# Gated attention plus Mish layer: another table of order rules, and another opening for the first K and Q

## The chip, the cores and the metric

The kernel runs on one core of one Trainium2 chip, in one launch. The metric is the device time of one execution in microseconds (us), and the median of the runs is what counts. The engines are named as in the profile: PE is TensorE's matrix unit (PEld its weight loads), DVE is VectorE, ACT is ScalarE, POOL is GpSimd, SP issues most DMAs. PSUM, where matmuls write, has eight banks of 512 float32 columns for each of its 128 partitions.

## The reference, cut to what matters

```python
def _A_ref(x, wqkv, wo):            # S = 2048 rows, D = 640, H = 32 heads of Dh = 20
    qkv = (x @ wqkv).reshape(B, S, 3, H, Dh) ...
    scores = einsum("bhqd,bhkd->bhqk", q, k) * Dh ** -0.5
    o = einsum("bhqk,bhkd->bhqd", softmax(scores), v)
    return o.reshape(B, S, D) @ wo
def _B_ref(x, w1, b1, w2):          # F = 1536
    h = x @ w1 + b1
    return (h * tanh(softplus(h))) @ w2          # Mish
g = sigmoid((x * gate_w).sum(-1, keepdims=True))
return g * _A_ref(A_x, ...) + (1 - g) * _B_ref(A_x, ...)
```

There are 32 heads x 2048 x 2048 scores, and each needs one exponential.

## The kernel before

**Units of work.** Heads are taken four at a time (`p`, 8 of them), queries 512 at a time (`qc`, 4 of them): 32 groups `G`. A group has 16 sets `j` of 128 keys, and a set has four score columns, one for each head, of 128 keys x 512 queries: 2048 columns in all, each one matmul (`score`, L1265) into one PSUM bank. Four such matmuls use different rows of the PE array (each 32 deep), so that several run side by side.

**Two ways to an exponential.** Most columns go to ScalarE: `emit_s` puts the scores of two or three columns into neighbouring banks and `emit_exp` (L1315) takes one ACTIVATE over them, a *pair* (1024 elements) or a *triple* (1536). The other sets are "drawn" for VectorE by `d_take`: `d_unit` (or `d_pair`, or two powers joined by `both`) writes scores into spare banks and `power_of` (L474) turns them into exponentials as an integer multiply and add whose bits are read as bf16. Such a set is used three times, with two shifted copies against rescaled values `VD`: a shift is one instruction on VectorE (L605) or four parts on GpSimd (L573). So a drawn set costs three value products where another set costs one.

**Value products.** `emit_pv` (L1358) issues four matmuls for a set, 21 columns of values and ones for each of the four heads, into four column strips of bank 7 (`acc`). When a group is complete, `normalise` transposes the sums on VectorE (L1380), takes reciprocals, multiplies on GpSimd (L1401) and stores the result for the last projection. The very last group is finished on VectorE alone (`ends`).

**Everything else is cut into chains.** Projections of q, k and v, the two matmuls of the Mish layer, the output projection and the transposes of x are `Chain` objects: lists of pieces (four matmuls side by side in four column strips of the array, L638) with an eviction by VectorE at the end. Mish itself is one ACTIVATE over 6144 elements, two in a batch, two batches (L926).

**What sets the order.** The program is straight-line, and the order on each engine is chosen when it is built, by a planner in the kernel's own Python: it steps a model clock, and `step_pe`, `step_act`, `step_dve` and `step_pool` choose the next instruction of each engine. On the chip each engine then runs its list in order, and waits on semaphores. `step_pe` decides by the fields of `rule` whether to issue the next scores (`S`), value products (`V`), a chain's piece (`F`) or scores for VectorE alone: for example how many banks to leave free (`KEEP3`), how many drawn sets may be open (`NOPEN`) or belong to one group (`LEAD`), how many ready value products are worth a change (`VMIN`, `PVMAX`), whether GpSimd takes a shift (`PS`, `PB`), whether two powers are joined (`MERGE`). `PLAN` (L175 and on) changes these fields while the work goes on; its keys are progress in groups, from 0 to 32:

```python
while plan and prog[0] >= plan[0]:
    vars(rule).update(PLAN[plan.pop(0)])
```

**The opening** is written by hand. Four row blocks of x are loaded on SP's and ScalarE's queues, then the weights of the first four heads (`load_first(1)` for K, `load_first(0)` for Q), `w_top` (48 more columns for K's padding) and `wv0` (the first value weights). x is transposed on TensorE, K's weights are padded into `wkp` (L366, L1474) and Q's into `wqp`, and ten matmuls for each make the first 512 columns of K and Q (L1484): for each of five row blocks of weights one matmul of 256 columns into one bank and one into another. VectorE copies one half (L1491), ScalarE the other (L1492). Then the first scores follow, and the planner's order begins.

**The end** is written by hand too: 24 matmuls for the last 512 rows (L1822), evictions and stores. `closing`, a flag, is set when the sums of the last group are transposed; while it is set, `step_dve` takes only work of the highest priority.

Of the kernel before, what the change touches and what calls it, by code (L numbers as in the profile page):

```python
# [9 lines left out]
P = 128  # L10
# [54 lines left out]
def kernel(  # L65
# [12 lines left out]
    nc = tc.nc  # L78
    _, S, D = A_x.shape
    F = B_w1.shape[1]  # L80
    H = 32
    DH = D // H
    KT = D // P
    FT = F // P
    NS = S // P
    QC = 512
# [88 lines left out]
    PLAN = {  # L175
        0.0: {'AHEAD': 5000.0, 'BEHIND': 6000.0, 'D2': 1.0, 'DQ': 2, 'DQ3': 0, 'DQ4': 0, 'ETIGHT': 1, 'HEAT': 0.7, 'HROOM': 100.0, 'KEEP3': 3, 'LEAD': 5, 'LOW': 0.5, 'MARGIN': 0.0, 'MERGE': 0, 'NEAR': 99, 'NOPEN': 5, 'PAIR': 0, 'PB': 3000.0, 'PS': 0, 'PVMAX': 4, 'Q3': 3, 'ROOM': 200.0, 'SWTH': 250.0, 'TWO': 9, 'VF': 0, 'VMIN': 1, 'WAIT1': 0.0, 'WAIT2': 6000.0, 'WAITU': 0.0},
        0.5: {'DQ4': 1, 'NEAR': 9, 'WAIT2': 100000.0},
        1.5: {'DQ3': 3, 'ETIGHT': 0, 'HEAT': 0.9, 'VMIN': 3},
        2.0: {'DQ4': 2, 'NEAR': 5, 'PS': 1, 'ROOM': 100.0, 'VMIN': 2, 'WAITU': 100000.0},
        2.5: {'AHEAD': 1000.0, 'Q3': 2},  # L180
        3.5: {'AHEAD': 2000.0, 'NEAR': 7, 'Q3': 3, 'SWTH': 520.0, 'WAIT1': -2000.0},
        4.0: {'MARGIN': 30.0, 'NEAR': 99, 'PVMAX': 2, 'VF': 2, 'VMIN': 1},
        4.5: {'ETIGHT': 1, 'TWO': 2, 'VMIN': 3},
        5.0: {'KEEP3': 1, 'LEAD': 4, 'LOW': 0.47, 'NOPEN': 4, 'Q3': 1, 'SWTH': 600.0, 'WAIT2': 3000.0},
        5.5: {'HROOM': -100.0, 'KEEP3': 3, 'LOW': 0.53, 'NEAR': 12, 'PVMAX': 3, 'VMIN': 2},
        6.0: {'PVMAX': 2},
        6.5: {'HEAT': 0.7, 'PS': 2},
        7.0: {'DQ3': 2, 'NOPEN': 5, 'TWO': 9, 'VMIN': 1},
        7.5: {'PB': 6000.0},
        8.0: {'LEAD': 6, 'WAIT2': 30000.0},  # L190
        8.5: {'HROOM': 100.0, 'MERGE': 1, 'NEAR': 9, 'Q3': 3, 'VF': 0, 'WAITU': -200000.0},
        9.0: {'D2': 0.5, 'HEAT': 0.8, 'MERGE': 0, 'WAITU': 100000.0},
        9.5: {'AHEAD': 3000.0, 'MERGE': 1, 'SWTH': 250.0, 'WAIT1': 0.0},
        10.0: {'PVMAX': 4, 'VF': 2},
        10.5: {'HEAT': 0.9},
        11.0: {'KEEP3': 1, 'ROOM': 300.0},
        11.5: {'KEEP3': 2, 'ROOM': 100.0},
        12.0: {'D2': 0, 'DQ': 1, 'LOW': 0.41, 'MERGE': 0, 'SWTH': 450.0},
        12.5: {'NOPEN': 3, 'Q3': 1},
        13.0: {'Q3': 3},  # L200
        14.0: {'HROOM': -200.0, 'LOW': 0.47, 'WAIT2': 100000.0},
        14.5: {'NOPEN': 2},
        15.0: {'HEAT': 0.7},
        15.5: {'HEAT': 0.9},
        16.0: {'DQ3': 0, 'DQ4': 0, 'HROOM': -100.0},
        17.0: {'PB': 3000.0},
        17.5: {'D2': 0.5, 'PB': 6000.0, 'TWO': 2},
        18.0: {'ROOM': 200.0},
        19.0: {'LOW': 0.6, 'NOPEN': 5},
        19.5: {'DQ3': 2, 'DQ4': 3, 'ETIGHT': 0, 'KEEP3': 1, 'LOW': 0.53, 'TWO': 1},  # L210
        20.0: {'DQ4': 1, 'MARGIN': 60.0, 'MERGE': 1, 'TWO': 2, 'WAIT1': -2000.0, 'WAITU': 0.0},
        20.5: {'NEAR': 99, 'PB': 3000.0, 'SWTH': 380.0},
        21.0: {'DQ4': 2, 'KEEP3': 3, 'NEAR': 7, 'PVMAX': 3},
        21.5: {'ETIGHT': 1, 'MERGE': 0, 'PB': 6000.0, 'Q3': 2, 'WAIT2': 30000.0},
        22.0: {'HROOM': 0.0, 'ROOM': 100.0},
        23.0: {'HROOM': -200.0, 'TWO': 1},
        23.5: {'PVMAX': 2},
        24.0: {'MARGIN': 30.0, 'NOPEN': 2, 'TWO': 9},
        25.0: {'NOPEN': 4, 'PB': 1500.0, 'PVMAX': 4, 'ROOM': 200.0, 'SWTH': 520.0, 'WAIT2': 100000.0},
        25.5: {'LEAD': 5, 'PB': 3000.0, 'WAIT2': 3000.0},  # L220
        26.0: {'HROOM': 100.0, 'ROOM': 100.0, 'TWO': 2},
        26.5: {'HROOM': -200.0, 'PVMAX': 2},
        27.0: {'KEEP3': 2, 'WAIT1': 0.0, 'WAITU': 100000.0},
        27.5: {'LOW': 0.44, 'PVMAX': 4, 'Q3': 3},
        28.0: {'DQ': 2, 'KEEP3': 3, 'MARGIN': 0.0},
        28.5: {'LOW': 0.38, 'TWO': 9, 'WAIT2': 30000.0},
        29.5: {'DQ': 1, 'DQ4': 1, 'NOPEN': 2, 'PS': 0, 'Q3': 1, 'WAIT2': 100000.0},
    }

    x2d = A_x[0]  # L230
# [9 lines left out]
    xT = consts.tile([P, KT, S], BF16, tag="xT")  # L240
    VA = consts.tile([P, NS, H, DH + 1], BF16, tag="VA")
    wv0 = work.tile([P, KT, 4 * DH + 1], BF16, tag="bl1", name="wv0")
# [7 lines left out]
    wqp = consts.tile([P, KT, 4, 32], BF16, tag="wqp")  # L250
    wkp = consts.tile([P, KT, 4, 32], BF16, tag="wkp")
# [4 lines left out]
    allb = psum.tile([P, 8, QC], F32, tag="Sp", name="Sp")  # L256
# [3 lines left out]
    def bank_ap(tag, shape, dtype=F32):  # L260
        ap = allb[:, tag, :]
        if dtype != F32:
            ap = ap.bitcast(dtype)
        if len(shape) == 3:
            return ap[:, 0 : shape[1] * shape[2]].rearrange("p (a b) -> p a b", b=shape[2])
        return ap[:, 0 : shape[1]]
# [9 lines left out]
    wrows = A_wqkv.rearrange("(kt p) c -> p kt c", p=P)  # L276
# [8 lines left out]
    KTOP = D - KPAD  # L285
# [9 lines left out]
    w_top = work.tile([P, KT, KPAD], BF16, tag="bl0", name="w_top")  # L295
# [20 lines left out]
        eng = nc.sync if u % 2 == 0 else nc.scalar  # L316
        eng.dma_start(out=xs[0][:, u, :], in_=x2d[u * P : (u + 1) * P, :])
    load_first(1, nc.sync)
    nc.scalar.dma_start(out=w_top[:, :, :], in_=wrows[:, :, D + KTOP : 2 * D])
    load_first(0, nc.scalar)  # L320
    nc.sync.dma_start(out=wv0[:, :, 0 : 4 * DH], in_=wrows[:, :, 2 * D : 2 * D + 4 * DH])

    def load_x(c):
        nc.sync.dma_start(  # L324
# [40 lines left out]
    def pad_copy(eng, dst, src):  # L365
        eng.tensor_copy(  # L366
            out=dst[:, :, :, 0:DH], in_=src.rearrange("p k (h d) -> p k h d", d=DH)
        )
# [4 lines left out]
    NG = len(groups)  # L373
# [16 lines left out]
    act_q = deque()  # L390
    pool_q = []
    two_port = [0.0]
    closing = [False]
    seq = [0]
    free = {"PE": 0.0, "ACT": 0.0, "DVE": 0.0, "POOL": 0.0}
    mode = [None]
# [975 lines left out]
    def normalise(G, ready):  # L1372
# [2 lines left out]
        st = {}  # L1375

        def a(t):
            closing[0] = G == NG - 1
            st["T1"] = work.tile([P, NS, 32], F32, tag=f"T1_{i}", name="T1")
            nc.vector.transpose(out=st["T1"][:, :, :].rearrange("p b r -> p (b r)"), in_=acc[:, :])  # L1380

# [30 lines left out]
        def ends(t):  # L1412
            st["O"] = work.tile([P, QC], BF16, tag=f"O{i}", name="O")
            for h in range(2):
                q = slice(h * QC // 2, (h + 1) * QC // 2)
                b_ = slice(h * NS // 2, (h + 1) * NS // 2)
                nc.vector.tensor_tensor(
                    out=T2[i][:, q].rearrange("p (b r) -> p b r", r=32)[:, :, 0:DH],
                    in0=st["T1"][:, b_, 0:DH],
                    in1=st["rec"][:, b_].unsqueeze(2).to_broadcast([P, NS // 2, DH]),  # L1420
                    op=ALU.mult,
                )
                nc.vector.transpose(out=st["O"][:, q], in_=T2[i][:, q])
            o_last[p] = st["O"]
            closing[0] = False

        def c_done(t):
            if kept:
# [46 lines left out]
        out=wkp[:, :, :, DH:32], in_=w_top[:, :, :].rearrange("p k (h d) -> p k h d", h=4)  # L1475
    )
    pad_copy(nc.vector, wqp, w_first[0][:, :, :])
    kT[0] = kTb[0]
    qT[0] = qTb[0]
    h_ = QC // 2  # L1480
    for w, dst, two in ((wkp, kT[0], (1, 4)), (wqp, qT[0], (5, 0))):
        for kt in range(KT):
            for h in range(2):
                nc.tensor.matmul(  # L1484
                    allb[:, two[h], 0:h_],
                    lhsT=w[:, kt, :, :].rearrange("p h d -> p (h d)"),
                    rhs=xT[:, kt, h * h_ : (h + 1) * h_],
                    start=(kt == 0),
                    stop=(kt == KT - 1),
                )  # L1490
        nc.vector.tensor_copy(out=dst[:, 0:h_], in_=allb[:, two[0], 0:h_])  # L1491
        nc.scalar.copy(out=dst[:, h_:QC], in_=allb[:, two[1], 0:h_])  # L1492
    for p in range(NQ - NSB, NQ):
        tag = "wqp" if p < NQ - 1 else f"wo{p}"
        wo_pad[p] = consts.tile([P, D], BF16, tag=tag, name=f"wo{p}")
# [236 lines left out]
    def step_dve(t):  # L1732
        best = None
        for it in dve_q:
            if it[1] <= t and (it[0] == 0 or not closing[0]) and (it[6] is None or it[6](t)):
                due = it[1] + (WAIT0, rule.WAIT1, rule.WAIT2, MWAIT)[it[0]]
                if it[0] == 3:
                    due = min(due, it[7] + WAIT3)
                if it[6] is not None and it[0] == 2 and cur["G"] > pv_G[0]:
                    due = min(due, it[1] + rule.WAITU)  # L1740
                rank = (due, it[2])
                if best is None or rank < best[0]:
                    best = (rank, it)
        if best is None:
            return None
        best = best[1]
        dve_q.remove(best)
        _, _, _, cost, fn, done, _, _ = best
        if rule.MERGE and best[2] in powers:
            o = beside(best, t)  # L1750
            if o:
                dve_q.remove(o)
                both(best, o, t)
                cost = 1134.0
                for x in (best, o):
                    x[5](t + cost + DVE_TAIL + SEM)
                return cost
        if best[0] == 2 and best[6] is not None:
            cost += max(free["POOL"] - t, 0.0)
            two_port[0] = t + cost  # L1760
        fn(t)
        if done:
            done(t + cost + DVE_TAIL + SEM)
        return cost
# [117 lines left out]
```

## Time and profile before

| | us |
|---|---|
| median of 3 runs (723.77 to 724.47) | 724.05 |
| the profiled execution: its time | 725.01 |
| the profiled execution: first to last instruction (span) | 723.2 |
| busy: PE / ACT / DVE / POOL | 706.3 / 704.3 / 619.6 / 430.4 |
| first exp starts / last exp ends | 9.67 / 714.45 |

Times within the profile are counted from the first instruction. "Busy" is the union of an engine's instructions; consecutive ones overlap on ACT and PE, so a busy engine can still have lost time: the step from start to start tells more than the duration. "Idle before" in a row is what the engine waited ahead of such instructions, with who ended the wait. The granted TensorE clock is 0.999 of full speed over the whole span.

### The profile page before, as it was taken

Reading aid. Unit: us, or ns where it says so; the run is one execution under the profiler, and the core shown is the slowest. Engines: PE = TensorE matmul, PEld = TensorE weight load, DVE = VectorE, ACT = ScalarE, POOL = GpSimd, SP = SyncE. Lnnn points to the kernel's source line nnn. Section 1 sums busy time; section 2 is a strip of 40 time slices with the busy share of each in tenths; the row PEclk is TensorE's granted clock in tenths of the full one; section 3 lists DMA queues with packets and bytes.
Section 4 is the critical chain, followed back from the end, with each engine's and each line's share of the span. In section 5 each row is a group of like instructions: output and inputs, shape, how many; then the busy total and the mean of one; then the engine's idle time right before and its main releaser. Section 6 shows DMA issues by size and latency. Waiting matters only on the chain.

```text
span 723.2 us, 24705 instructions
## 1 busy us (share of the span) xinstructions
PE 706.3 (98%) x10256; PEld 232.5 (32%) x10256; DVE 619.6 (86%) x1042; ACT 704.3 (97%) x735; POOL 430.4 (60%) x697
## 2 busy tenths in 40 slices
PE   8899999999999999999999999999999999999997
PEld 4433332222222443332332222222243333333332
DVE  5389999887788779889988899898889988988997
ACT  6899999999999999999999999999999999999996
POOL 2002675565797767778787778667984456663000
PEclk9999999999999999999999999999999999999999
DMA  9511122122321201111131223231231131132111
GB/s 246 178 22 38 30 56 44 33 62 59 85 43 32 68 27 28 14 32 27 50 84 34 41 47 70 60 67 38 44 57 31 34 50 35 29 60 45 20 36 38
DMA packets 123313, 37.87 MB, mean 52 GB/s; under 512 B 90880, under 2 KB 122640, under 8 KB 123200
## 3 DMA queue, kind: packets, MB, share of 16 engines
q1 hardware_dynamic: 121600, 35.80, 22.8%
q8 instruction: 80, 1.31, 0.7%
q10 hardware_dynamic: 1600, 0.49, 0.3%
q14 instruction: 33, 0.27, 0.1%
HBM read 22.29 MB, written 11.48 MB: 47 GB/s over the span
## 4 chain that ended last, share of the span: by engine, by line
PE 62%; ACT 23%; issue 5%; DVE 4%; SPq 2%; DMA 2%; POOL 0%; ACTq 0%; POOLq 0%
PE Sp L1265 22%; ACT E L1315 20%; PE Sp L1358 20%; PE Sp L638 20%; DVE T L474 2%; ACT big L926 1%; DMA w_sb<-in_B_w_dram 1%; DVE T L605 1%; SPq L291 1%; SPq L304 1%; DMA big<-in_A_x_dram 1%; PE Sp L1822 0%; SPq L708 0%; SPq L324 0%; ACT L1315 0%
## 5 line engine op out<-in xcount | busy, mean ns | idle before, releaser
L1315 ACT ACTIVATE E<-Sp 128x1024 bf16<-128x1024 f32 x717 | 672.6, 1077 | 6.3 <-PE Sp L1265 5.9
L573 POOL TENSOR_TENSOR T<-T,step_t 128x256 int32<-128x256 int32 x652 | 401.1, 649 | 107.9 <-PE Sp L1358 71.5
L474 DVE TENSOR_SCALAR T<-Sp 128x512 int16<-128x512 f32 (+1 forms) x587 | 389.1, 686 | 62.3 <-PE Sp L1265 57.7
L1265 PE MATMUL Sp<-qT,kT 32*128 32x512 bf16 x2048 | 290.9, 384 | 8.0 <-ACT E L1315 3.7
L1265 PEld LDWEIGHTS <-kT 32*128 32x128 bf16 x2048 | 74.5, 91 | 267.0 <-issue 262.0
L1358 PE MATMUL Sp<-E,VA 128*21 128x512 bf16 x1456 | 138.0, 383 | 0.4 <-DVE T L1380 0.4
L1401 POOL TENSOR_TENSOR T<-T,rec 128x320 bf16<-128x320 f32 x31 | 25.1, 809 | 167.0 <-DVE rec L1394 140.0
L1358 PE MATMUL Sp<-T,VD 128*21 128x512 bf16 x1184 | 112.2, 382 | 0.5 <-DVE T L605 0.5
L605 DVE TENSOR_SCALAR T<-T 128x2048 int16<-128x2048 int16 x133 | 105.2, 797 | 1.5 <-PE Sp L1358 0.5
L638 PE MATMUL Sp<-xT,w1t 128*32 128x512 bf16 x960 | 76.8, 383 | 0.2
L638 PE MATMUL Sp<-w_sb,big 128*32 128x320 bf16 x1536 | 74.3, 301 | 0.3 <-DVE st L742 0.3
L1358 PEld LDWEIGHTS <-VA 128*21 128x21 bf16 x2048 | 44.4, 90 | 72.5 <-issue 64.5
L1358 PE MATMUL Sp<-T,VA 128*21 128x512 bf16 x592 | 57.4, 383 | 0.0
L638 PE MATMUL Sp<-xT,ws 128*32 128x512 bf16 x720 | 55.9, 382 | 0.5 <-DVE T L474 0.5
L638 PEld LDWEIGHTS <-big 128*32 128x32 bf16 x1536 | 35.4, 96 | 25.9 <-issue 15.8
L1358 PEld LDWEIGHTS <-VD 128*21 128x21 bf16 x1184 | 28.4, 90 | 37.6 <-issue 32.2
L892 DVE TENSOR_SCALAR big<-Sp,b1f 128x512 bf16<-128x512 f32 x48 | 35.6, 742 | 2.1 <-PE Sp L638 1.9
L638 PE MATMUL Sp<-wv,xT 128*32 128x81 bf16 (+2 forms) x960 | 34.6, 258 | 1.3 <-DVE T L474 1.3
L638 PE MATMUL Sp<-wo_sb,od 128*32 128x320 bf16 (+1 forms) x608 | 32.3, 302 | 0.0
L742 DVE CAST st<-Sp 128x512 bf16<-128x512 f32 x36 | 24.5, 681 | 5.3 <-PE Sp L638 5.3
L638 PEld LDWEIGHTS <-w1t 128*32 128x32 bf16 x960 | 19.0, 94 | 26.3 <-issue 22.4
L826 DVE CAST VA<-Sp 128x80 bf16<-128x80 f32 (+2 forms) x48 | 16.2, 372 | 10.1 <-PE Sp L638 10.1
(74 smaller groups left out, 205.7 us busy)
## 6 DMA issues: line engine op xcount, KB each, us to landing
w1t<-in_B_w_dram SPq DMA_DIRECT2D x24, 320.0 KB
q_dram<-st SPq DMA_DIRECT2D x20, 128.0 KB
out_dram<-ot SPq DMA_DIRECT2D x16, 160.0 KB
qT<-q_dram SPq DMA_DIRECT2D x124, 20.0 KB
o_dram<-T SPq DMA_DIRECT2D x120, 20.0 KB
kT<-k_dram SPq DMA_DIRECT2D x28, 80.0 KB
k_dram<-st SPq DMA_DIRECT2D x16, 128.0 KB
big<-in_A_x_dram SPq DMA_DIRECT2D x3, 640.0 KB
```

The costliest lines, as they stand in the source:

```text
L291: eng.dma_start(out=t[:, :, :], in_=wrows[:, :, c0 : c0 + P])
L474: nc.vector.tensor_scalar(out=dst.bitcast(I16), in0=src, scalar1=inv_sqrt_dh * LOG2E * 128.0, scalar2=127.0 * 128.0 + BETA, op0=ALU.mult, ...
L573: nc.gpsimd.tensor_tensor(out=tile_[:, :].bitcast(I32)[:, k * n : (k + 1) * n], in0=d["T"][:, :].bitcast(I32)[:, k * n : (k + 1) * n], in1 ...
L605: nc.vector.tensor_scalar(out=tile_[:, :].bitcast(I16), in0=d["T"][:, :].bitcast(I16), scalar1=float(SHIFT[i]), scalar2=None, op0=ALU.add,)
L638: nc.tensor.matmul(out_[k : k + 32], lhsT=lhsT[:, k : k + 32], rhs=rhs, tile_position=(0, k), **kw)
L742: nc.vector.tensor_copy(out=res["st"][:, :], in_=ps[:, :])
L826: nc.vector.tensor_copy(out=VA[:, sts[i], h0 : h0 + nh, 0:DH], in_=ps[:, i, 0:n].rearrange("p (h d) -> p h d", d=DH),)
L892: nc.vector.tensor_scalar(out=big[:, slot.tag, (ft % 2) * QC : (ft % 2 + 1) * QC], in0=ps[:, :], scalar1=b1f[:, ft : ft + 1], scalar2=None ...
L1265: nc.tensor.matmul(ps_cols, lhsT=kT[p][32 * t_ : 32 * t_ + 32, j * P : (j + 1) * P], rhs=qT[G][32 * t_ : 32 * t_ + 32, :], tile_position=( ...
L1315: nc.scalar.activation(E[:, x : x + n, :], ps, ACT.Exp, scale=inv_sqrt_dh,)
L1358: nc.tensor.matmul(acc[32 * t_ : 32 * t_ + DH + 1, :], lhsT=lhsT, rhs=rhs, start=(pv_done[G] == 0), stop=(pv_done[G] == pv_total[G] - 1), ...
L1401: nc.gpsimd.tensor_tensor(out=T2[i][:, :].rearrange("p (b r) -> p b r", r=32)[:, :, 0:DH], in0=st["T1"][:, :, 0:DH], in1=st["rec"][:, :].u ...
```

## The change

`PLAN` is replaced from progress 1.0 on (the entries for 0.0 and 0.5 stay). `closing` goes. In the opening, `w_top` is loaded on SP's queue behind K's weights, and the first value weights on ScalarE's queue behind Q's; K and Q are made by five matmuls of 512 columns each, into one bank each (6 and 2), and both engines copy their half out of that bank. Line numbers move by 6 (L1265 becomes L1271) and by 4 near the end.

```diff
-        1.5: {'DQ3': 3, 'ETIGHT': 0, 'HEAT': 0.9, 'VMIN': 3},
-        2.0: {'DQ4': 2, 'NEAR': 5, 'PS': 1, 'ROOM': 100.0, 'VMIN': 2, 'WAITU': 100000.0},
-        2.5: {'AHEAD': 1000.0, 'Q3': 2},
...
-        29.5: {'DQ': 1, 'DQ4': 1, 'NOPEN': 2, 'PS': 0, 'Q3': 1, 'WAIT2': 100000.0},
+        1.0: {'DQ4': 3, 'VMIN': 2, 'WAITU': 100000.0},
+        1.5: {'DQ4': 2, 'PS': 2, 'PVMAX': 3},
+        2.0: {'DQ4': 1, 'PS': 1, 'PVMAX': 4, 'VF': 1, 'WAIT1': -2000.0},
...
+        31.5: {'BEHIND': 3000.0, 'DQ4': 1, 'ETIGHT': 0, 'HROOM': 100.0, 'LEAD': 5},
...
     load_first(1, nc.sync)
-    nc.scalar.dma_start(out=w_top[:, :, :], in_=wrows[:, :, D + KTOP : 2 * D])
     load_first(0, nc.scalar)
-    nc.sync.dma_start(out=wv0[:, :, 0 : 4 * DH], in_=wrows[:, :, 2 * D : 2 * D + 4 * DH])
+    nc.sync.dma_start(out=w_top[:, :, :], in_=wrows[:, :, D + KTOP : 2 * D])
+    nc.scalar.dma_start(out=wv0[:, :, 0 : 4 * DH], in_=wrows[:, :, 2 * D : 2 * D + 4 * DH])
...
-            closing[0] = G == NG - 1
...
-            closing[0] = False
...
+    sb = [bank_ap(g, [P, QC]) for g in (6, 2)]
     kT[0] = kTb[0]
     qT[0] = qTb[0]
-    h_ = QC // 2
-    for w, dst, two in ((wkp, kT[0], (1, 4)), (wqp, qT[0], (5, 0))):
+    for w, dst, k in ((wkp, kT[0][:, 0:QC], 0), (wqp, qT[0][:, :], 1)):
         for kt in range(KT):
-            for h in range(2):
-                nc.tensor.matmul(
-                    allb[:, two[h], 0:h_],
-                    lhsT=w[:, kt, :, :].rearrange("p h d -> p (h d)"),
-                    rhs=xT[:, kt, h * h_ : (h + 1) * h_],
-                    start=(kt == 0),
-                    stop=(kt == KT - 1),
-                )
-        nc.vector.tensor_copy(out=dst[:, 0:h_], in_=allb[:, two[0], 0:h_])
-        nc.scalar.copy(out=dst[:, h_:QC], in_=allb[:, two[1], 0:h_])
+            nc.tensor.matmul(
+                sb[k][:, :],
+                lhsT=w[:, kt, :, :].rearrange("p h d -> p (h d)"),
+                rhs=xT[:, kt, 0:QC],
+                start=(kt == 0),
+                stop=(kt == KT - 1),
+            )
+        h_ = QC // 2
+        nc.vector.tensor_copy(out=dst[:, 0:h_], in_=sb[k][:, 0:h_])
+        nc.scalar.copy(out=dst[:, h_:QC], in_=sb[k][:, h_:QC])
...
-            if it[1] <= t and (it[0] == 0 or not closing[0]) and (it[6] is None or it[6](t)):
+            if it[1] <= t and (it[6] is None or it[6](t)):
```

What the two programs hold, as their lists of instructions show (no time is in these):

| engine, instruction | before | after |
|---|---|---|
| ACT exp over 1024 / 1536 / 512 | 693 / 23 / 1 | 688 / 24 / 0 |
| DVE power over 512 / over 1024 | 582 / 5 | 578 / 11 |
| DVE shift / POOL parts of shifts | 133 / 652 | 135 / 660 |
| PE sets of four value matmuls | 808 | 812 |
| PE runs of scores; of these with five or more | 711; 5 | 713; 2 |
| PE matmuls for the first K and Q | 20 of 256 columns | 10 of 512 columns |

From the 24th run of scores on, the order of TensorE differs, and with it the others.

## The prediction

> **What bounds the kernel now.** I read the page's busy shares first, then ScalarE's groups by form, its timeline, the waits from 50 us on, TensorE's timeline, and last the opening.
>
> ```profile
> PE 706.3 (98%) x10256; PEld 232.5 (32%) x10256; DVE 619.6 (86%) x1042; ACT 704.3 (97%) x735; POOL 430.4 (60%) x697
> ```
>
> Two engines are full at once. ScalarE's time is nearly all exps, and its groups split them by width:
>
> ```profile
> L1315 ACT ACTIVATE E<-Sp 128x1024 bf16<-128x1024 f32 x693 | 644.4, 1064 | 6.2 <-PE Sp L1265 5.9 <-PE Sp L1358 0.2
> L1315 ACT ACTIVATE E<-Sp 128x1536 bf16<-128x1536 f32 x23 | 34.2, 1487 | 0.1
> ```
>
> 693 pairs take 644.4 us, 0.930 each. One takes 1.064 from its start to its end, so neighbours overlap, and a late start of up to 0.13 us is not idle time. ScalarE's timeline gives the step when nothing is late:
>
> ```profile
> 669.92 9.27 ACT L1315 ACTIVATE E<-Sp 128x1024 bf16<-128x1024 f32 x10
> 705.65 8.80 ACT L1315 ACTIVATE E<-Sp 128x1024 bf16<-128x1024 f32 x9
> ```
>
> Ten pairs in 9.27: less the last one's 1.08, nine steps of 0.91. The second line, by the list of the order, is six pairs, two triples and the single: (8.80 - 0.67 - 6 x 0.91) / 2 = 1.34 for a triple. Over all pairs (0.930 - 0.910) x 693 = 13.9 us are lost to late scores, besides 6.2 us of open idle, most of it before 50 us: there the ACT waits after 50 us name only this.
>
> ```profile
> ACT E L1315 <- PE Sp L1265: 0.7, 3, 0.4
> ```
>
> So ScalarE is the bound, and TensorE has next to no room to be early. Its prices stand in its timeline, as differences of starts:
>
> ```profile
> 707.26 0.46 PE L638 MATMUL Sp<-wo_sb,od 128*32 128x320 bf16 x8
> 707.55 0.39 PE L1358 MATMUL Sp<-T,VD 128*21 128x512 bf16 x4
> 707.87 0.39 PE L1265 MATMUL Sp<-qT,kT 32*128 32x512 bf16 x3
> 708.19 0.40 PE L1358 MATMUL Sp<-E,VA 128*21 128x512 bf16 x4
> 708.42 0.39 PE L1358 MATMUL Sp<-T,VD 128*21 128x512 bf16 x4
> 708.74 0.39 PE L1265 MATMUL Sp<-qT,kT 32*128 32x512 bf16 x3
> ```
>
> A set of four value matmuls takes 0.22 and another 0.10 if scores follow; a run of two to four scores takes 0.32; a group of four 320-wide ones 0.14 (8 in 0.29). A run of scores with both changes is thus 0.42, and 0.93 leaves some 0.5 for other work. Priced so, and with 0.22, 0.10 and 0.07 for groups of 512, 240 and 81 columns, the order holds 683.1 us of TensorE work against 662.0 us of exps (693 x 0.91 + 23 x 1.34 + 0.6) and 26.3 us of Mish (four of 5.3 and four table loads of 1.28), 688.3 together. ScalarE is the fuller by 5.2 us; beyond that, time is lost where one exp's slot is overfull on TensorE and the next is not.
>
> **The change, part by part.** The sums go against the profiled execution, 725.01 us with a span of 723.2; the median of the three runs, 724.05, is 0.96 lower, and the difference is carried over to it.
>
> *Exps.* By the lists of both orders: pairs 693 to 688, triples 23 to 24, the single gone: -5 x 0.930 + 1.34 - 0.67 = -4.0 us on ScalarE. These eight score columns go to VectorE (592 to 600 columns: sets drawn off ScalarE 148 to 150).
>
> *TensorE.* Two more sets mean four more value sets, 808 to 812: 4 x 0.22 = 0.9. Runs of scores 711 to 713: 2 x 0.42 = 0.8. Runs of five and more, which pay twice inside, 5 to 2: -0.6, and some regrouping. The whole list gives 683.7, +0.6. At steps without loss ScalarE comes down to 688 x 0.91 + 24 x 1.34 + 26.3 = 684.5: the two are level.
>
> *VectorE.* 582 to 578 single powers (-4 x 0.681), 5 to 11 double ones (+6 x 1.216), two more shifts (+2 x 0.797): +6.2 on 619.6, that is 87%. It waits 55.1 us for scores after 50 us, which hides this; if that cover is gone, 6.2 is the most it costs. *GpSimd:* +8 x 0.649 = 5.2 us on 60%, hidden by 107.9 us of idle before such parts; else the shift is late for its value set, not for an exp.
>
> *What of the 4.0 reaches the end.* I cut both lists behind every exp and added up, piece by piece, the larger of TensorE's work and ScalarE's steps (Mish left out in both; no wait is carried from piece to piece): 717.7 before, 715.1 after (-2.6). With cuts behind every second, third and fourth exp the change is -2.9, -1.3 and -3.8; behind every eighth -0.6, every sixteenth -0.2, every 24th +0.4. Short pieces fit the kernel, which keeps two exps' scores ahead, and they average -2.65; since work can also be moved a little, I take -2.3, and the ends for the range are +0.4 and -4.0.
>
> *The opening.* It ends at 9.67 with the first exp, and it is serial:
>
> ```profile
> 6.06 0.22 DVE L1474 COPY wkp<-w_top 128x240 bf16<-128x240 bf16 x1
> 6.34 1.30 PE L1484 MATMUL Sp<-xT,wkp 128*128 128x256 bf16 x10 [0.22 <-DVE wkp L1474]
> 7.52 1.27 PE L1484 MATMUL Sp<-xT,wqp 128*128 128x256 bf16 x10
> 8.71 0.42 DVE L1491 CAST qT<-Sp 128x256 bf16<-128x256 f32 x1 [0.71 <-PE Sp L1484]
> 8.82 0.37 ACT L1492 CAST qT<-Sp 128x256 bf16<-128x256 f32 x1 [0.77 <-PE Sp L1484]
> 9.24 0.40 PE L1265 MATMUL Sp<-qT,kT 32*128 32x512 bf16 x4 [0.46 <-ACT qT L1492]
> ```
>
> The two copies of Q run side by side out of two banks. In the changed program both read one bank, and the list with its waits shows ScalarE's copy waiting for VectorE's, no longer for TensorE. The Trainium skill, "PSUM — Partial Sum Buffer", section "PSUM bank collisions raise a hardware error", says that two engines must not read one bank and quadrant at once, and that readers are included. By that rule the wait is needed and the sum stays as follows; without it the copies could run side by side and the opening would cost 0.5 less. No run here shows two engines on one bank. Price: VectorE's copy now needs all columns (8.71 becomes about 8.85), 0.42, a hand-over of about 0.06, 0.37: scores at about 9.75 instead of 9.24, +0.5. K's copies serialise too, under Q's matmuls. Ten weight loads fewer and 512 columns a matmul cost the same columns: 0, at best -0.2.
>
> w_top's load moves from ScalarE's queue, where it is issued at 1.65 behind two x loads, to SP's behind K's weights, and so to about 2.12, where the list has the value weights now. Its landing is not shown; the first weight block, issued at 1.65, is used unwaited at 5.85, 4.2 later, so about 6.3; the latest is wqp's 7.20, the landing of a block issued at 2.14. So the copy at 6.06 is late by 0 to 1.1; I take 0.2, nearest to the first. Q's weights come sooner, but Q waits for K on TensorE (7.52 follows 7.51). The gate's and values' weights move to ScalarE's queue and are wanted at 11.98: nothing. The x loads on SP stand behind a smaller block: nothing. Opening in sum +0.7, bounds +0.3 and +1.6.
>
> *The tail.* `closing` held back VectorE's other work during the last normalisation; the changed list has none left after the last transpose of the sums, but one wo eviction (0.54) just before. The last exp is a pair (1.06, was 0.67), while the shifts that held TensorE at 714.97 are gone. 0, bounds -0.4 and +0.4.
>
> Sum: -2.3 + 0.7 = -1.6: 723.4 for a profiled execution, **722.4** for the median.
>
> **Rivals.** *Full relief* (0.17): lost time stays at 0.020 a pair, the whole 4.0 comes off: 724.05 - 4.0 + 0.7 = 720.8. For it: ScalarE is the fuller engine and TensorE's list grows by only 0.6. Against it: then both are level, and every full slot counts.
>
> *TensorE becomes the bound, in uneven slots* (0.38). In pieces of 24 exps its surplus over ScalarE grows from 24.4 to 27.4 us. If that can't be moved out of its stretch, it is paid as late scores, and the exps removed were not what was waited for: 724.05 + 3.0 + 0.7 = 727.8. It decides from the point where the mean busy time of a pair passes 0.930 + (4.0 - 0.7) / 688 = 0.935, and is slower for certain above 0.937. For it: the order is another one from the 24th run of scores on, and TensorE's waits after 50 us (3.3 us for exps) leave no reserve. Against it: short pieces all shrink.
>
> *That the rules change nothing* can't be: the lists differ in nearly every line from there on.
>
> **How the numbers follow.** This kernel's runs differ by 0.7 us, and 0.2% (1.45 us) is about what can be told from no change: faster is below 722.6, slower above 725.5. The forecast (0.45) lies at the edge of faster: 0.26 faster, 0.14 same, 0.05 slower, since its terms have ends of -4.0 to +0.4 and +0.3 to +1.6; its own range is 720 to 726. Full relief gives 0.16 and 0.01; the uneven slots 0.04 same and 0.34 slower. Faster 0.42, same 0.19, slower 0.39. The range reaches below the full relief by the 2.8 us that fewer late scores could give, and above the slower rival by 0.9 for a late w_top and 0.4 for the tail: 718.0 to 729.1.
>
> **What would show it.** Right: ScalarE's pairs 688 at 0.925 to 0.935 busy each, triples 24, first exp at 10.2 to 10.6, ScalarE's copy of Q starting where VectorE's ends. Wrong: pairs above 0.937 (late scores), open ACT waits after 50 us well over 1 us, a first exp after 11 (w_top), or TensorE waiting for VectorE's powers by several us, where double powers hold two banks for 1.2 us.

## The result, and the profile after

The changed kernel takes 721.09 us (median of 20 runs, 720.49 to 724.94); the kernel before, measured beside it, 724.39 (20 runs, 723.53 to 728.46). The ratio is 0.9952, with an interval of 0.9942 to 0.9962: faster by 3.3 us by the medians, 3.5 by the ratio, half a per cent. The profiled executions stand at 725.01 before (span 723.2) and 721.08 after (span 719.3), 3.9 apart; the one of before lies above its three timed runs (723.77 to 724.47), so a part of the 3.9 may be that execution's own.

Busy time of the engines, from the page of the changed kernel:

```profile
PE 704.2 (98%) x10262; PEld 234.2 (33%) x10262; DVE 626.0 (87%) x1046; ACT 700.2 (97%) x730; POOL 440.9 (61%) x705
```

ScalarE's groups by form (count | busy, mean ns of one | idle before, with who ended it):

```profile
L1321 ACT ACTIVATE E<-Sp 128x1024 bf16<-128x1024 f32 x688 | 640.5, 1078 | 5.6 <-PE Sp L1271 3.8 <-PE Sp L1364 1.1
L1321 ACT ACTIVATE E<-Sp 128x1536 bf16<-128x1536 f32 x24 | 36.6, 1523 | 0.4 <-PE Sp L1271 0.4
```

A pair takes 640.5 / 688 = 0.931 us of busy time; before it was 0.930. The exps that went took their full price with them, and a pair loses no more to late scores than before. All exps together, where overlaps count once, are busy 668.6 us after 672.6, so -4.0.

The waits from 50 us on, ScalarE's and TensorE's (total, times, longest):

```profile
PE Sp L1271 <- ACT E L1321: 1.8, 8, 0.4
PE Sp L1364 <- DVE T L1385: 1.3, 2, 0.8
ACT E L1321 <- PE Sp L1364: 1.1, 2, 0.9
ACT E L1321 <- PE Sp L1271: 0.9, 3, 0.4
```

and TensorE's longest group before:

```profile
PE Sp L1265 <- ACT E L1315: 3.3, 10, 0.5
```

TensorE waits less for exps to free a bank (1.8 us against 3.3), and up to the last exp neither engine waits longer than 0.9 us at once.

The opening, from the timeline (start, duration, engine, line, then the idle time and who ended it):

```profile
6.60 0.22 DVE L1478 COPY wkp<-w_top 128x240 bf16<-128x240 bf16 x1 [0.77 <-DMA w_top<-in_A_wqkv_dram]
6.88 1.25 PE L1487 MATMUL Sp<-xT,wkp 128*128 128x512 bf16 x5 [1.14 <-DVE wkp L1478]
9.32 0.42 DVE L1495 CAST qT<-Sp 128x256 bf16<-128x256 f32 x1 [0.72 <-PE Sp L1487]
9.78 0.37 ACT L1496 CAST qT<-Sp 128x256 bf16<-128x256 f32 x1 [0.78 <-DVE qT L1495]
10.20 0.40 PE L1271 MATMUL Sp<-qT,kT 32*128 32x512 bf16 x4 [0.99 <-ACT qT L1496]
```

The copy of `w_top` starts at 6.60, not at 6.06, and waits for its load. ScalarE's copy of Q starts 0.46 behind VectorE's and waits for it. The first exp starts at 10.62 instead of 9.67. Other executions with the same opening scatter: 10.54 to 11.06 in the five of e2, e6, e8, e9 and e10, and 9.47 to 10.11 in the five others with the old one (e1, e5, e7, e11, e12).

The whole stretch from the first exp's start to the last one's end (length, then busy time of PE, PEld, DVE, ACT and POOL with counts, granted clock, DMA share, GB/s):

```profile
10.62:711.06 700.44, 692.94 (x10194) 228.53 (x10194) 616.71 (x1023) 694.83 (x721) 435.67 (x691) 1.00 0.23 50
```

It was 704.78 long (9.67 to 714.45). So the 3.9 us divide into +0.95 ahead of the first exp, -4.34 in this stretch, and -0.51 behind the last exp (8.75 to 8.24: the first transpose of the last sums starts 0.48 after the last exp's end, where it was 1.01).

### The profile page after: what moved, and what is told of

Read it like the earlier page. It is cut to its first block, busy times and chain, and to the rows that moved or that the text cites. A ratio compares the mean times of both kernels' runs of the same rounds, so it can differ in the third digit from the quotient of the medians.

```text
span 719.3 us, 24738 instructions
## 1 busy us (share of the span) xinstructions
PE 704.2 (98%) x10262; PEld 234.2 (33%) x10262; DVE 626.0 (87%) x1046; ACT 700.2 (97%) x730; POOL 440.9 (61%) x705
## 4 chain that ended last, share of the span: by engine, by line
PE 67%; ACT 23%; issue 5%; DVE 2%; DMA 1%; SPq 0%; ACTq 0%; DVEq 0%
PE Sp L1271 24%; PE Sp L644 22%; ACT E L1321 21%; PE Sp L1364 21%; ACT big L932 1%; DVE T L480 1%; DMA kT<-k_dram 1%; DMA w_top<-in_A_wqkv_dram 1%; DVE T L611 0%; PE Sp L1487 0%; DVE st L748 0%; ACT L1321 0%; ACT L932 0%; SPq L777 0%; DVE VD L431 0%
## 5 line engine op out<-in xcount | busy, mean ns | idle before, releaser
L1321 ACT ACTIVATE E<-Sp 128x1024 bf16<-128x1024 f32 (+1 forms) x712 | 668.6, 1093 | 6.0 <-PE Sp L1271 4.2
L579 POOL TENSOR_TENSOR T<-T,step_t 128x256 int32<-128x256 int32 x660 | 409.7, 655 | 157.4 <-PE Sp L1364 92.3
L480 DVE TENSOR_SCALAR T<-Sp 128x512 int16<-128x512 f32 (+1 forms) x589 | 395.9, 693 | 56.6 <-PE Sp L1271 50.2
L1271 PE MATMUL Sp<-qT,kT 32*128 32x512 bf16 x2048 | 286.5, 384 | 6.2 <-ACT E L1321 2.2
L1271 PEld LDWEIGHTS <-kT 32*128 32x128 bf16 x2048 | 76.7, 91 | 264.6 <-issue 259.0
L1406 POOL TENSOR_TENSOR T<-T,rec 128x320 bf16<-128x320 f32 x31 | 27.1, 875 | 89.8 <-DVE rec L1399 78.3
L644 PE MATMUL Sp<-w_sb,big 128*32 128x320 bf16 x1536 | 76.4, 301 | 0.5 <-DVE T L480 0.4
L644 PEld LDWEIGHTS <-xT 128*32 128x32 bf16 x960 | 17.9, 96 | 16.4 <-issue 14.3
```

Of the source, the lines that this page charges most:

```text
L480: nc.vector.tensor_scalar(out=dst.bitcast(I16), in0=src, scalar1=inv_sqrt_dh * LOG2E * 128.0, scalar2=127.0 * 128.0 + BETA, op0=ALU.mult, ...
L579: nc.gpsimd.tensor_tensor(out=tile_[:, :].bitcast(I32)[:, k * n : (k + 1) * n], in0=d["T"][:, :].bitcast(I32)[:, k * n : (k + 1) * n], in1 ...
L644: nc.tensor.matmul(out_[k : k + 32], lhsT=lhsT[:, k : k + 32], rhs=rhs, tile_position=(0, k), **kw)
L1271: nc.tensor.matmul(ps_cols, lhsT=kT[p][32 * t_ : 32 * t_ + 32, j * P : (j + 1) * P], rhs=qT[G][32 * t_ : 32 * t_ + 32, :], tile_position=( ...
L1321: nc.scalar.activation(E[:, x : x + n, :], ps, ACT.Exp, scale=inv_sqrt_dh,)
L1406: nc.gpsimd.tensor_tensor(out=T2[i][:, :].rearrange("p (b r) -> p b r", r=32)[:, :, 0:DH], in0=st["T1"][:, :, 0:DH], in1=st["rec"][:, :].u ...
```

## The experiments

Two theories stand against each other. **A:** the time follows ScalarE's list: fewer exps, each at its old price. **B:** it follows the sum over short pieces of the order, the larger of TensorE's work and ScalarE's steps in each (the *slot sum* of the prediction: 717.7 before, 715.1 after), and with it how evenly TensorE's work lies between the exps. Beside them stands a question on the opening: whether its later first exp is paid at the end. The expectations give further rivals where they are met. The kernel before was run on the same chip each time (medians 724.67, 725.0 and 724.98 for the three groups of experiments, e1 to e4, e5 to e8, e9 to e12). The record also has each run's mean granted clock. The lower it is, the longer the run, and kernels differ in how many of their runs it lowers; so beside the medians of all runs some medians of the runs at 0.999 or more are given below, called *full-clock* runs. They pick runs by something that the kernel itself can bring about, and are few, so they count as a second view and not as the result.

### e1: the new rules with the old opening

```diff
 (from the changed kernel)
     load_first(1, nc.sync)
+    nc.scalar.dma_start(out=w_top[:, :, :], ...)
     load_first(0, nc.scalar)
-    nc.sync.dma_start(out=w_top[:, :, :], ...)
-    nc.scalar.dma_start(out=wv0[:, :, 0 : 4 * DH], ...)
+    nc.sync.dma_start(out=wv0[:, :, 0 : 4 * DH], ...)
...
-    sb = [bank_ap(g, [P, QC]) for g in (6, 2)]
+    # K in banks 1 and 4, Q in 5 and 0, 256 columns each, as before
```

> The new rules with the opening of before (two banks for each of the first K and Q, w_top on ScalarE's queue). Theory A (the gain is ScalarE's shorter list, and every exp follows the opening): the first exp starts at 9.7 instead of 10.6 and the whole follows, 721.1 - 0.9 = 720.2, ratio to before 0.994. Rival B (the early order waits for loads anyway: late scores at 17, 26, 35 and 44 us): the 0.9 is given back before 50 us, 720.9 to 721.1. Rival C (the new rules fit only with a later start): above 721.5.

Measured: 721.7 us (12 runs, 719.76 to 725.37), ratio 0.9961 (0.9939 to 0.9983). By this median it lies in rival C's range. The first exp starts at 9.51, and still the median isn't better than that of the changed kernel. The full-clock runs say otherwise: 720.44 for e1 (6 of its 12 runs), 723.76 for before (16 of 35), 721.00 for the changed kernel (16 of 20, measured at another time). There the rules are worth 3.3 us, and the new opening costs some 0.6 with them, near theory A. Five runs of e1 stand at a clock of 0.997 or less (722.69 to 725.37), only two of the changed kernel's 20. TensorE's waits in its profile show loads where the changed kernel has next to none (0.2 us):

```profile
PE Sp L1271 <- DMA kT<-k_dram: 1.6, 1, 1.6
PE Sp L1271 <- DMA qT<-q_dram: 1.1, 1, 1.1
```

The first is at 186 us, and TensorE's clock behind it shows why it costs more than its 1.6 us. The windows (as above; the clock is the third figure from the end):

```profile
186.00:188.20 2.20, 0.65 (x10) 0.09 (x2) 1.07 (x2) 1.87 (x3) 1.75 (x3) 1.00 0.39 125
188.20:190.00 1.80, 1.79 (x12) 0.32 (x12) 1.00 (x2) 0.00 (x0) 0.00 (x0) 0.59 0.03 14
190.00:192.00 2.00, 2.00 (x22) 0.54 (x19) 0.38 (x1) 1.45 (x1) 0.00 (x0) 0.51 0.00 0
192.00:194.00 2.00, 2.00 (x28) 0.53 (x25) 1.41 (x3) 1.64 (x2) 0.00 (x0) 1.00 0.00 0
```

For 3.41 us TensorE runs at half clock. So what an earlier start gains can be lost again to a load. At 34 us TensorE is 1 us earlier than in the changed kernel (the value products ahead of Q's scores start at 32.52 against 33.57), and Q's load is issued 1.6 us later (32.66 against 31.07). At 186 us TensorE is no longer early (scores at 186.26 against 186.03), and K's load is issued only 0.2 later (180.35 against 180.13), but the scores behind it start 1.6 later (188.21 against 186.64): there the load itself took longer. Why isn't shown.

### e2: the new opening with the old rules

```diff
 (from the kernel before; its PLAN and `closing` stay)
-    nc.scalar.dma_start(out=w_top[:, :, :], ...)
     load_first(0, nc.scalar)
-    nc.sync.dma_start(out=wv0[:, :, 0 : 4 * DH], ...)
+    nc.sync.dma_start(out=w_top[:, :, :], ...)
+    nc.scalar.dma_start(out=wv0[:, :, 0 : 4 * DH], ...)
...
+    sb = [bank_ap(g, [P, QC]) for g in (6, 2)]
+    # K in bank 6 and Q in bank 2, 512 columns each, as changed
```

> The old rules with the new opening. Theory A: the first exp at 10.6, and 724.4 + 0.9 = 725.3, ratio 1.0013. Rival B (loads are waited for anyway before 50 us): 724.4 to 724.7. If the new opening itself were what gained, 721 to 723.

Measured: 724.88 us (12 runs, 724.23 to 726.28) against 724.67, ratio 0.9999 (0.9982 to 1.0016). The first exp starts at 10.79, 1.12 later than before, and the span is 723.3, as before (723.2). The windows from 35 to 50 us show where it is taken back between these two executions, of the kernel before:

```profile
35.00:50.00 15.00, 13.58 (x268) 5.43 (x267) 12.51 (x29) 12.88 (x16) 0.00 (x0) 1.00 0.13 26
```

and of e2:

```profile
35.00:50.00 15.00, 13.75 (x277) 5.52 (x273) 12.78 (x29) 14.27 (x17) 0.00 (x0) 1.00 0.12 23
```

ScalarE is busy 14.27 us here instead of 12.88 (+1.39), after 11.05 instead of 11.57 up to 20 us and 14.04 instead of 14.67 up to 35 (-1.15 in all). In the kernel before, TensorE waits 0.8 us at 34 us for the second Q:

```profile
PE Sp L1265 <- DMA qT<-q_dram: 0.8, 1, 0.8
```

In e2 that wait is gone. In this pair of executions the opening's delay used time that a load needed anyway. It doesn't hold for all runs: the full-clock runs of e2 stand at 724.42 (6 of 12) against 723.76 for before, +0.7, and the interval of all runs, about -1.3 to +1.2 us, has room for that too. So these runs show no gain from the opening, and a cost of 0 to 0.7 us at the end; the gain of the change is that of the rules.

### e3 and e4: one half of the opening each

e3, two banks as before, `w_top` on SP's queue as changed:

```diff
-    sb = [bank_ap(g, [P, QC]) for g in (6, 2)]
+    # K in banks 1 and 4, Q in 5 and 0, 256 columns each, as before
```

> The changed kernel, but K and Q in two banks each, so that the two engines copy side by side; w_top stays on SP's queue. If ScalarE's wait for VectorE's copy costs 0.46 (9.32 to 9.78 in the trace of after): first exp at about 10.1, 720.6. If w_top alone sets the start, no change: 10.6, 721.1.

e4, one bank as changed, `w_top` and the value weights on their old queues:

```diff
+    nc.scalar.dma_start(out=w_top[:, :, :], ...)
     load_first(0, nc.scalar)
-    nc.sync.dma_start(out=w_top[:, :, :], ...)
-    nc.scalar.dma_start(out=wv0[:, :, 0 : 4 * DH], ...)
+    nc.sync.dma_start(out=wv0[:, :, 0 : 4 * DH], ...)
```

> The changed kernel, but w_top first on ScalarE's queue and the value weights on SP's, as before; one bank each stays. If the 0.77 wait for w_top's landing is what it costs: VectorE's copy of w_top runs right behind the one of K's weights, K's matmuls start 0.5 to 0.7 earlier, first exp at 9.9 to 10.1, 720.4 to 720.6. If Q's weights, then issued second, take its place as the late block: 10.4 to 10.6, 721.1.

Measured: e3 721.46 us (12 runs, 719.52 to 725.84), ratio 0.9962 (0.9936 to 0.9989); e4 720.49 (12 runs, 719.56 to 725.57), ratio 0.9945 (0.9928 to 0.9962). The totals can't be told from each other or from the changed kernel. (In e4 eleven of the twelve runs are full-clock runs, with a median of 720.35.) The first exps differ. e3's timeline:

```profile
10.29 1.02 ACT L1321 ACTIVATE E<-Sp 128x1024 bf16<-128x1024 f32 x1 [0.48 <-PE Sp L1271]
```

and e4's:

```profile
6.21 1.25 PE L1487 MATMUL Sp<-xT,wkp 128*128 128x512 bf16 x5 [0.41 <-DVE wkp L1478]
9.96 1.02 ACT L1321 ACTIVATE E<-Sp 128x1024 bf16<-128x1024 f32 x1 [0.48 <-PE Sp L1271]
```

In these executions the second bank is worth 0.33 us at the first exp (10.62 to 10.29; expected was about 10.1), the queue of `w_top` 0.66 (10.62 to 9.96; expected 9.9 to 10.1). Both stand below the 10.54 to 11.06 of the new opening's executions, e3 by 0.25 only, so the sizes are rough.

### e5 and e6: narrower exps

The exps cover 496 of each 512 columns; the other 16 are set once to 1.0 and stay. Scores and value products are as they were.

```diff
+    NX = 496
+    nc.gpsimd.memset(E[:, :, NX:QC], 1.0)
...
-            E[:, x : x + n, :], ps, ACT.Exp, scale=inv_sqrt_dh,
+            E[:, x : x + n, 0:NX], ps[:, :, 0:NX], ACT.Exp, scale=inv_sqrt_dh,
```

With the old rules:

> The kernel before, with every exp over 496 of a bank's 512 columns (16 queries of each exp left out). A pair's step shrinks by 32 x 0.84 ns (from 1.34 and 0.91), ScalarE's list by 19.6 us, TensorE's stays at 683 of work. If ScalarE alone is the bound: 724.4 - 19.6 = 704.8. If the two engines bound it slot by slot: half of it or less, 714 to 718; the surplus of 5.2 over TensorE comes off first. If TensorE were the bound already: above 722.

With the new rules:

> The same cut in the changed kernel (16 queries of each exp left out). ScalarE alone: 721.1 - 19.5 = 701.6. If the new order has made the engines level, less is gained here than under the old rules, by up to 4 us: 714 to 718 as well, and the two kernels end within 1 us of each other. If it gains as much as the old one, the order is not nearer to TensorE's limit than before.

Measured: e5 724.63 us (10 runs, 721.06 to 727.56), ratio 0.9993 (0.9973 to 1.0014); e6 716.99 (4 runs, 716.54 to 717.21), ratio 0.9895 (0.988 to 0.991). ScalarE's list is 19.5 us shorter at steps without loss. ScalarE's pairs, first of e5, then of e6:

```profile
L1317 ACT ACTIVATE E<-Sp 128x992 bf16<-128x992 f32 x693 | 637.3, 1006 | 13.5 <-PE Sp L1267 9.2 <-ACT E L1317 0.2 <-PE Sp L1360 0.2
```

```profile
L1323 ACT ACTIVATE E<-Sp 128x992 bf16<-128x992 f32 x688 | 630.5, 1013 | 8.7 <-PE Sp L1273 3.9 <-PE Sp L1366 1.4 <-ACT E L1323 0.4
```

A pair has 32 columns less, but its busy time falls only to 0.920 in e5 and 0.916 in e6: most of the 19.5 us turns into waiting for scores. In e5 even the rest is lost in many runs (five of ten have a mean clock of 0.997 or less, none of e6's four). In its profile Q's second load isn't there when TensorE comes to it:

```profile
35.11 1.06 PE L1267 MATMUL Sp<-qT,kT 32*128 32x512 bf16 x2 [1.66 <-DMA qT<-q_dram]
```

It waits 1.66 us and then runs at half clock for 10.24 us. e5's profile stands at 725.89 with a mean clock of 0.993; its lowest runs, 721.06 and 721.78, are at the full clock and lie 2.2 to 3.0 us below the full-clock runs of before on that chip (724.02). So in the old order a lighter ScalarE is worth 3 us at most, and in the new one 721.09 - 716.99 = 4.1 for the same 19.5. e6 lies in its range of 714 to 718, but the expectation that less would be gained there than in the old order didn't come true; e5's median lies in the range for a TensorE that already is the bound.

### e7 and e8: shorter value products

The value products cover 480 of a group's 512 queries, except for the group's first set: TensorE has 10.3 us less to do, and the sums of the last 32 queries are incomplete.

```diff
+        nv = QC if pv_done[G] == 0 else 480
...
-                acc[32 * t_ : 32 * t_ + DH + 1, :],
+                acc[32 * t_ : 32 * t_ + DH + 1, 0:nv],
...
-                rhs=rhs,
+                rhs=rhs[:, 0:nv],
```

With the old rules:

> The kernel before, with the value products over 480 of 512 queries, all but a group's first set (the other 32 queries' sums are left out): TensorE has 776 x 13 ns = 10.3 us less, ScalarE the same. If ScalarE is the bound and late scores are only a part: -1 to -3, 721.4 to 723.4. If TensorE is the bound: -8 to -10, 715. If the lost time has nothing to do with TensorE's load: 724.4.

With the new rules:

> The same cut in the changed kernel (32 queries' sums left out). If the engines are level now, more is gained here than under the old rules: -3 to -5, 716 to 718. If ScalarE is still the bound as it was: -1 to -3, 718 to 720.

Measured: e7 722.39 us (10 runs, 720.95 to 725.01), ratio 0.9971 (0.9957 to 0.9985); e8 716.62 (4 runs, 716.26 to 716.78), ratio 0.9891 (0.9875 to 0.9908). Of TensorE's 10.3 us, 2.1 to 2.6 reach the end with the old rules (against the interval's middle and against the median of before), 4.5 with the new ones (721.09 - 716.62). e7 lies in the range for a ScalarE that is the bound, e8 in the one for two levelled engines. That isn't the only reading: seven of e7's ten runs have a mean clock of 0.997 or less, none of e8's four, so in the old order a part of the gain may be lost to loads and the clock, as in e5 (e7's two full-clock runs, 720.95 and 721.92, lie 2.1 to 3.1 us below before's 724.02). And in the new order ScalarE's share has grown as well (e6), so that levelling alone doesn't explain the four.

### e9 and e10: half of the table each

e9 takes the new rules up to progress 16 and the old ones, in full, from there; e10 the reverse.

```diff
 (e9, from the changed kernel; e10 with the halves exchanged)
-        16.0: {'DQ3': 3, 'HEAT': 0.9, 'NEAR': 5, 'NOPEN': 5, 'WAIT2': 30000.0},
...
+        16.0: { all fields as the old rules have them at 16.0 },
+        17.0: {'PB': 3000.0},
...
```

> The changed kernel with the new rules up to progress 16 and the state and entries of the old ones from there on. Its lists hold 683 pairs, 31 triples and a single: ScalarE 690.0 us (before 688.3, after 684.5), TensorE 681.9, and the sum of the larger per exp is 717.1 (before 717.7, after 715.1). Theory A (ScalarE's list carries through): before + 1.7, with the new opening 725.5 to 726.5. Theory B (the fit of TensorE's work to each exp's slot): as before, 724 to 725. Theory C (the gain was made in the first half): 721 to 722.

> The reverse: old rules up to progress 16, new ones behind. 662 pairs, 44 triples: ScalarE 687.7 us (0.6 less than before), TensorE 677.4 (5.7 less), but the sum of the larger per exp is 726.2 (8.5 more than before; in pieces of two and three exps 6.5 and 8.8 more). Theory A: 723.5 to 724. Theory B: slower than before, 728 to 733. If TensorE's total were the bound: 719 to 720.

Measured: e9 727.12 us (11 runs, 726.77 to 729.08), ratio 1.0028 (1.0014 to 1.0042); e10 737.81 (5 runs, 736.37 to 739.63), ratio 1.0174 (1.0139 to 1.021). Neither half of the table is good by itself. By their lists, as differences to before:

| kernel | ScalarE's list | slot sum | measured |
|---|---|---|---|
| changed | -3.8 | -2.6 | -3.3 |
| e9 | +1.7 | -0.6 | +2.1 |
| e10 | -0.6 | +8.5 | +12.8 |

All three have the new opening. e9 is slower though its slot sum is smaller: theory A, if 0.6 above its range (725.5 to 726.5); with the 0.6 to 0.7 us that the opening costs in full-clock runs its +2.1 is about accounted for. e10 is slower though ScalarE has less to do: theory B, and by more than the range of B (728 to 733). Its ACT waits from 50 us on say where:

```profile
ACT E L1320 <- PE Sp L1363: 11.9, 5, 4.2
```

The longest of them, 4.2 us, lies behind this stretch of its timeline (only the scores, the chains' pieces and the late exp are kept):

```profile
640.23 0.39 PE L1270 MATMUL Sp<-qT,kT 32*128 32x512 bf16 x3
...
640.78 0.85 PE L643 MATMUL Sp<-wo_sb,od 128*32 128x320 bf16 x20
...
641.46 1.80 PE L643 MATMUL Sp<-w_sb,big 128*32 128x320 bf16 x48
...
643.30 1.53 PE L643 MATMUL Sp<-wo_sb,od 128*32 128x320 bf16 x40
...
645.14 1.94 ACT L1320 ACTIVATE E<-Sp 128x1024 bf16<-128x1024 f32 x2 [4.18 <-PE Sp L1363]
...
645.41 0.39 PE L1270 MATMUL Sp<-qT,kT 32*128 32x512 bf16 x3
```

From 640.23 to 645.41 TensorE issues no scores but 108 matmuls of chains. They are no backlog of the first half of the rules: when half of all scores are issued, 2664 of the 4844 chain matmuls are done in e10 and 2656 in the changed kernel. Why the second half bunches them here isn't shown. The three rows fit both theories as halves of one: where either ScalarE's list or the slot sum rises, the time rises with it, and where both fall, it falls. Three kernels don't make a formula of it, and in the changed kernel, where both fall, they can't be told apart.

### e11 and e12: the loads that TensorE runs into

e1 had shown that the new order loses time to loads. e11 has the old opening and takes w2's load of 1.9 MB out of SP's queue ahead of them, to a later place; e12 also issues the loads of the next K right behind the store that they read, ahead of four stores to `o_dram` and a w1 load that SP's queue had in front of them. TensorE's, VectorE's, ScalarE's and GpSimd's lists in e12 are those of e1.

```diff
 (e11, from e1)
-    nc.sync.dma_start(out=w2_sb[:, :, :], ...)        # behind the first loads
...
+        nc.sync.dma_start(out=w2_sb[:, :, :], ...)    # with the gate's values
 (e12, besides)
-        for k in range(4):
-            r0 = p * HF + k * DH
-            nc.sync.dma_start(out=kTb[p % NLAST][32 * k : 32 * k + DH, :], in_=k_dram[r0 : r0 + DH, :])
+    def issue_k(t):      # the same four loads, as soon as K's rows are stored
+                         # and the buffer's last scores are done
...
```

> New rules with the opening of before, and the load of w2 (1.9 MB) moved from the opening to the gate's event at about 43 us, where it still is long ahead of its use. If the wait at 34 us for Q's second load comes from SP's queue standing behind w2's landing (3.5 to 4.8 us at the first store of K's top rows), the wait goes, and with it the drop of the granted clock behind it: late scores before 50 us 5.4 to about 4, 719.5 to 720.2. If the wait comes from the store of Q itself: no change, 720 to 721.7.

> The same, and K's loads for the third and fourth four heads issued right behind the store that they read, ahead of four stores of the output and a load of w1 on SP's queue. If the wait at 186 us (0 to 2.5 us from run to run, and a granted clock of 0.5 for 3.4 us behind it) comes from that queue: it is gone in every run, 719.0 to 719.8, and the spread of the runs falls under 1.5 us. If the load's own landing is what is late: as e11.

Measured: e11 721.01 us (11 runs, 719.61 to 723.39), ratio 0.9948 (0.9928 to 0.9969). The wait at 34 us is gone, as expected, though the median stays in the range for no change (720 to 721.7); the one at 186 us stands in its profile, 2.3 us long, again with half clock for 3.41 us behind it. e12: 719.56 us (5 runs, 718.78 to 719.58), ratio 0.9918 (0.9891 to 0.9944), in its expected range, with the lowest median and the smallest spread of all versions with the whole computation. TensorE's waits in its profile, the longest groups:

```profile
PE Sp L1280 <- ACT E L1330: 2.4, 11, 0.4
PE Sp L1373 <- DVE T L1394: 1.3, 2, 0.8
PE Sp L363 <- DVE qT L361: 1.2, 1, 1.2
```

No load is left among them, and its five runs lie within 0.8 us instead of 5.6 (e1, 12 runs), all at a clock of 0.999 or more. Whether the old opening's earlier first exp comes through better here was not tried by itself. Its interval touches that of the changed kernel, and the two were measured at different times, so the distance between them (1.5 us by medians) is an estimate.

## Why the prediction was right, and where not

The direction and the range held, and the forecast of 722.4 lies 1.3 us above the measured median. That says little by itself: the range was 11 us wide, and faster had a chance of 0.42 against 0.39 for slower. By its steps:

- **ScalarE's list, -4.0:** right; exps are busy 668.6 us after 672.6.
- **TensorE +0.6, VectorE +6.2, GpSimd +5.2, all hidden:** right in that none of it reaches an exp. VectorE grew by the forecast amount (626.0 after 619.6), GpSimd by twice it (440.9 after 430.4). From 50 us on TensorE waits longer for VectorE's transposes of the sums (1.3 us after 0.4), but less for VectorE in all (2.0 after 2.8), and no late exp lies behind these waits. TensorE's list can't be read from its busy time, where waits are inside (706.3 to 704.2).
- **What of the 4.0 reaches the end, -2.3:** mis-sized. In the profile the stretch of exps shrank by 4.34. Part of that isn't the rules': the opening's delay is taken back there before 50 us (e2). In the full-clock runs of e1 the rules are worth -3.3, and -3.0 by the medians of all runs. The term came from an average of the pieces' sums in which regrouped work must lose a part of the gain; what the profile shows is nearer to the other rival's mechanism, *full relief*: a pair's mean stays where it was, 0.931. Its price, 720.8, lies 0.3 from the result, with some luck: it takes off 4.0 where the rules gave about 3.3, and starts from 724.05 where the kernel before now stood at 724.39.
- **The opening, +0.7:** its size at the first exp was nearly right, +0.95: `w_top` late by 0.54 (said 0.2, bounds 0 and 1.1), the copies of Q in series 0.46 (said 0.5). What reaches the end isn't settled: e2 gives +0.2 us by all its runs with an interval of about -1.3 to +1.2, and +0.7 in full-clock runs, as forecast. The term left out that TensorE may wait behind the opening for something that the opening doesn't delay; it does, for Q's second load at 34 us, 0.8 us in the profiled execution of before, and there the delay cost nothing.
- **The tail, 0 (bounds -0.4 and +0.4):** -0.51 in the profile, outside by 0.1.
- **Uneven slots, 727.8:** not in this kernel. The pairs' mean stayed below 0.935. That such a mechanism exists and what it costs, e10 shows: 737.81.
- **"ScalarE is the bound":** too simple. e5 shows that 19.5 us less on ScalarE is worth at most 3 in the old order; that TensorE's list is only 5.2 us shorter fits that. For the 4.0 us of this change it held, in an order whose slot sum is smaller too.

What stays open: which entries of `PLAN` make the gain, since only halves of the table were tried; whether the shorter list or the smaller slot sum made it; why e10 loses 4.3 us more than its slot sum; what the opening costs at the end, between 0 and 0.7; and whether one or two banks in it matter to the total (e3). No run takes `closing` away alone. In the changed kernel's trace VectorE does nothing but the last normalisation between its first transpose at 711.54 and the last one's end at 714.28, so the flag would have had nothing to hold back there.

## What to carry to other kernels

When two engines are full within one per cent, ask of a new order two things: does the longer list get shorter, and does the other engine's work still fit between its steps; the time got worse where either did. A later start can be taken back where TensorE would have waited for a load anyway, and an earlier one can be lost there; so look for the next load wait before either is charged to the end. And where the granted clock differs from run to run, compare the kernels also at one clock: the medians of all runs show nothing here of the 0.6 to 0.7 us that the later start costs in full-clock runs. Rules picked for a whole course hold for that course: half of a good table was worse than the old one.

## What the runs showed of the hardware

An idle time of TensorE well below the length of the half-clock stretch is enough to bring it about. In e1, 1.56 us of waiting for K (PE busy 0.65 of 2.20 us) was followed by a granted clock of 0.5 for 3.41 us; in e11, 2.3 us by the same 3.41; in e5, 1.66 us by 10.24, three times as long. The 0.8 us at 34 us in the kernel before brought none, nor did 1.3 us of waiting for K in e3 and in e6. The Trainium skill, "TensorE: Matmul & The Clock Gate", section "What's actually happening", gives a free-running window of 3413 ns and calls the array cold after an idle window of some 3.4 us; by its section "HAM oscillation — how this bites in real kernels" gaps have to be longer than about 3.4 us. The length of the window agrees with these runs. The length of the gap doesn't: here 1.6 us, with TensorE partly busy around it, did.

The traces say more. In all of them, each stretch at one clock that ends before the program does lasts a whole number of pieces of 3.413 us (30.72 us is 9 of them, 184.32 is 54). Cut into such pieces from the first stretch on, TensorE is busy in the piece right ahead of a drop for 1.86 us (e1, 185.11 to 188.53), 1.74 (e11), 1.79 (e5), at most 2.08 (e10, at 720.61). The emptiest pieces at full clock with no drop behind them have 2.11 (e5, at 717.74) and 2.18 (e9, at 536.31); e3's, which holds most of its wait of 1.30 us, has 2.40. So in these 14 traces, with some 2900 such pieces, the busy time within a piece tells the drops from the rest, at about 2.1 of 3.413 us, and the length of one gap doesn't. Why e5's half clock lasts three pieces, with TensorE busy for 10.20 of 10.24 us, isn't shown.

The spread among runs of one kernel, some 5 us, goes with the clock: e1's seven runs at a mean granted clock of 0.998 or more take 719.76 to 722.11 us, the five at 0.997 or less 722.69 to 725.37. e12, in whose profile TensorE waits for no load, has five runs within 0.8 us, all at 0.999 or more. That waits for loads lower the clock in the runs without a profile too is likely, but argued.
